# A retention and two-layer feed-forward kernel on one core: the sign of float64 weights found another way, and attention block loads split over two DMA queues

## Chip, core, metric

The kernel runs on one core of one Trainium2 chip. The metric is device microseconds (us) of one execution; the median of three runs is given, and one more execution was profiled. Engines are named as in the profile: PE (matrix multiply), PEld (its weight loads), DVE (vector engine), ACT (scalar engine), POOL (GpSimd), SP (the engine that does nothing here but issue DMAs).

## Reference

The weights are float64, everything else is float32.

```python
def _attn_ref(q, k, v):                       # B=2, H=8, S=768, D=64
    gamma = 1.0 - 2.0 ** (-5.0 - np.arange(H))
    for t in range(S):
        state = gamma * state + k[:, :, t] (outer) v[:, :, t]
        y[:, :, t] = q[:, :, t] @ state / sqrt(D)

def _moe_ref(x, w_in, w_out):                 # x 1536 x 512, w_in 512 x 2048, w_out 2048 x 512
    h = x @ w_in
    return (np.maximum(h, 0.0) + np.log1p(np.exp(-np.abs(h)))) @ w_out

def _moe2_ref(x, w_in, w_out):                # same shapes
    h = x @ w_in
    return (h * np.clip(h + 3.0, 0.0, 6.0) / 6.0) @ w_out

out = _moe2_ref(_moe_ref(attention(q, k, v)))
```

## The kernel before

**Matrix products.** Each layer m (0 or 1) is worked off in steps s = (m, c, f): c is one of 3 chunks of 512 tokens, f one of 16 slices of 128 of the hidden width, 96 steps in all. `gemm1` makes h for a step in one PSUM bank (12 matmuls of 512 columns), ACT and DVE make the activation g from it and split it into a high part `hi` and a low part `lo`, and `gemm2` adds the step's share of the output into four PSUM banks (12 matmuls). A product of two float32 numbers is three products of parts: high by high, high by low, low by high. After the last f of a chunk, ACT and DVE split the four banks into `x_hi` and `x_lo`, the input of the next layer. Below, "a product" is one such group of 12 matmuls.

**Weights.** There are 64 weight tiles (32 a layer), each 128 x 512 float64, 512 KB. `weight(m, o, f, number)` loads one into a `raw` buffer as two 32-bit words for each number and makes the parts in a `cv` buffer: `bits` (ACT) turns the low word into the mantissa's last bits; `sign` (ACT) reads the top 16 bits of the high word and writes a float16 zero with the right sign into the upper half of the same word; the high word, read as a float32, is then scaled by 2^-112 and clamped, either `scale` on ACT and `clamp` on DVE (all of layer 1, and every second tile of layer 0, by `SCALED`) or `scaled` and `capped`, both on DVE (the other 16 tiles of layer 0); `merge` (DVE) shifts it by three bits and ORs it into `cv`. `high` (ACT), and `low` (DVE) or `negative` (ACT) with an accumulating DMA that POOL issues, then write the two parts into a `w` buffer.

**Attention.** The 12 units u of 128 positions come in three kinds. Units 0 to 3 run first. Units 4 to 7 are spread between the first products of layer 0. Units 8 to 11 are spread between later ones, when the 32 weights of layer 0 are done and their `raw` and `cv` buffers serve as attention buffers. For these last four, k and q are loaded as 32 x 32 blocks (`blocks`: 16 DMAs of 16 KB for `kb`, 16 for `qb`), DVE transposes each (`in_blocks`), and q is multiplied by a table. There is one `kb`, one `qb`, one `kT` and one `qT` buffer, so a unit's blocks can be loaded only when DVE has transposed those of the unit before. A unit is three groups of small matmuls on PE: scores S, inner and state products I, and carry C.

**Order.** Nothing is scheduled at run time: each engine works its instructions off in the order written. The class `Plan` writes that order. Every task has an engine, a cost in microseconds, a due time, the tasks that it waits for and the buffers that it takes; the planner takes the task that could start first, or one that could start within `NEAR` of it and is due earlier. A changed cost or dependency so changes the order on all engines, PE's too.

```python
found.append((at, t))
...
first = min(a for a, _ in found)
at, t = min(((a, t) for a, t in found if a <= first + self.NEAR[e]), key=lambda x: (x[1].due, x[1].n))
```

All instructions are recorded under line 44, the helper through which the planner issues them; tiles tell them apart.

Of the kernel before, what the change touches and what calls it, by code (L numbers as in the profile page):

```python
# [10 lines left out]
F32 = mybir.dt.float32  # L11
F32R = mybir.dt.float32r
U32 = mybir.dt.uint32
U16 = mybir.dt.uint16
F16 = mybir.dt.float16
AF = mybir.ActivationFunctionType
ALU = mybir.AluOpType
PSUM = bass.MemoryType.PSUM
P = 128
# [106 lines left out]

PSX, TT, TS, ACP, ACS = 0.61, 0.62, 0.36, 0.49, 0.55
GEMM = 2.73


@with_exitstack
def kernel(ctx, tc, q, k, v, w1_in, w1_out, w2_in, w2_out, table, out):
    nc = Plan(tc)
    B, H, S, D = q.shape
# [4 lines left out]
    NF = DFF // P  # L139
# [12 lines left out]
    HOLD = 8.0  # L152
# [2 lines left out]
    def BY_DVE(n):  # L155
        return n < 6 or n < 2 * NF and n % 4 != 0

    def SCALED(n):
        return n >= 2 * NF or n % 2 == 1

    tc.nc.scalar.preload_act_table_set("softplus")

# [3 lines left out]
    fixed = pool("fixed")  # L166
# [12 lines left out]
    hold = holds.enter_context(tc.tile_pool(name="hold", bufs=1))  # L179
# [42 lines left out]
    half = fixed.tile([P, 1], F32, name="half")  # L222
    three = fixed.tile([P, 1], F32, name="three")
    nc.vector.memset(half, -0.5 + 7.5 * 2.0 ** -12)
    edge = fixed.tile([P, 1], F32, name="edge")
    nc.vector.memset(three, 3.0)
    nc.vector.memset(edge, 32767.5 * 2.0 ** -60)


    G = [(m, c, f) for m in range(2) for c in range(NC) for f in range(NF)]  # L230
    cost = {"Tk": 0.46, "Tq": 0.46, "S": 0.60, "D": 0.60, "C": 0.98, "I": 0.60, "S0": 0.97, "D0": 0.57, "I0": 0.97, "C0": 0.97, "G1": GEMM, "G2": GEMM}
    pe = [("Tk", 0), ("Tq", 0)]
# [12 lines left out]
    n = 0  # L245
# [6 lines left out]
    due, t = {}, 5.0  # L252
# [10 lines left out]
    def w_part(key, i):  # L263
        return at_slot(("w", key))[:, i]

    def weight(m, o, f, number):
        key = m, o, f
        made = conv[0] if m == 0 else []
        use = due[("G2" if o else "G1"), min(m * NC * NF + f, len(G) - LAG)] - 4.0

        def raw():
            return at_slot((f"raw{m}", key))

        def low_word():
            return raw()[:, :, 0]

        def y():
            return raw()[:, :, 1]

        def w():  # L280
            return at_slot((f"cv{m}", key))

        def fetch():
            src = words[m][o]
            if o:
                nc.sync.dma_start(out=raw().rearrange("p n t -> p (n t)"), in_=src[f * P:(f + 1) * P, :])
            else:
                nc.sync.dma_start(out=raw().rearrange("p (k n) t -> p k (n t)", k=KD),
                                  in_=src[:, 2 * f * P:2 * (f + 1) * P].rearrange("(k p) f -> p k f", p=P))

        def bits():
            nc.scalar.activation(w(), low_word(), AF.Relu, scale=2.0 ** -29 * (1 - 2.0 ** -12), bias=half)

        def sign():
            top = raw().bitcast(U16)[:, :, 3]
            to = w().bitcast(F16).rearrange("p (n x) -> p n x", x=2)[:, :, 1]
            nc.scalar.activation(to, top, AF.Identity, scale=-2.0 ** -60, bias=edge)

        def scale():
            nc.scalar.activation(y().bitcast(F32), y().bitcast(F32), AF.Copy, scale=2.0 ** -112)  # L300

        def clamp():
            nc.vector.tensor_scalar(y().bitcast(F32), y().bitcast(F32), -TOP, TOP, ALU.max, ALU.min)

        def scaled():
            nc.vector.tensor_scalar(y().bitcast(F32), y().bitcast(F32), 2.0 ** -112, -TOP, ALU.mult, ALU.max)

        def capped():
            nc.vector.tensor_scalar(y().bitcast(F32), y().bitcast(F32), TOP, None, ALU.min)

        def merge():
            nc.vector.scalar_tensor_tensor(w(), y(), 3, w(), ALU.logical_shift_left, ALU.bitwise_or)

        def high():
            nc.scalar.activation(w_part(key, 0), w().bitcast(F32), AF.Copy)

        def negative():
            nc.scalar.activation(w_part(key, 1), w().bitcast(F32), AF.Copy, scale=-1.0)

        def low():  # L320
            nc.vector.tensor_tensor(w_part(key, 1), w().bitcast(F32), w_part(key, 0).bitcast(F32), ALU.subtract)

        def add():
            nc.gpsimd.dma_start(out=w_part(key, 1).bitcast(F32), in_=w().bitcast(F32), accum_op=ALU.add)

        raw_k, cv_k = (f"raw{m}", key), (f"cv{m}", key)
        cv, part = [(f"cv{m}", cv_k)], [("w", ("w", key))]
        tail = 1.5 if BY_DVE(number) else 7.0
        T["F", key] = t0 = nc.add("SP", 0.45, fetch, due=begin + 15 if number < 1 else use - tail - 8.0, take=[(f"raw{m}", raw_k)], load=1.45 if o else 1.75)
        t1 = nc.add("ACT", 0.65, bits, [t0], use - tail - 3.5, take=cv)  # L330
        t2 = nc.add("ACT", 0.57, sign, [t1], use - tail - 2.9)
        if SCALED(number):
            t3 = nc.add("ACT", 0.57, scale, [t2], use - tail - 2.3)
            t4 = nc.add("DVE", TS, clamp, [t3], use - tail - 1.9)
        else:
            t3 = nc.add("DVE", TS, scaled, [t2], use - tail - 2.3)
            t4 = nc.add("DVE", TS, capped, [t3], use - tail - 1.9)
        t5 = nc.add("DVE", TT, merge, [t4, t2], use - tail - 1.3, give=[raw_k])
        if BY_DVE(number):
            a = nc.add("ACT", ACS, high, [t5], use - 1.5, take=part, give=[cv_k] + made)  # L340
            b = nc.add("DVE", TT, low, [a], use - 0.7, give=[cv_k] + made)
        else:
            n = nc.add("ACT", ACS, negative, [t5], use - tail, take=part)
            b = nc.add("POOL", 0.9, add, [n], use - tail + 1, give=[cv_k] + made, load=1.6)
            a = nc.add("ACT", ACS, high, [n], use - 2.5, give=[cv_k] + made)
        T["W", key] = [a, b]
# [37 lines left out]
    for j in range(2):  # L384
        r = slice(j * HALF, (j + 1) * HALF)
# [3 lines left out]
        nc.tensor.transpose(idle[:, i % NP, :], ident, ident)  # L389

    arena = [("arena", j) for j in range(LATE)]

    part = [slice(j * HALF, (j + 1) * HALF) for j in range(2)]

# [26 lines left out]
    def attend(u):  # L421
        b, i = divmod(u, NCH)
        ph = int(u >= FIRST)
        d = {n: due.get((n, u)) for n in cost}
# [3 lines left out]
        def task(eng, cost, fn, after, when, take=(), give=(), load=0.0, hold=0.0):  # L428
            when -= EDGE * (u < START and eng in ("DVE", "ACT"))
            return nc.add(eng, cost, fn, after, when, [(p, k) for p, k in take], list(give) + mine, load, hold)  # L430

        def tile_of(n):
            return at_slot((n, u))

        def own(n):
            return [(f"{n}{ph}", (n, u))]
# [9 lines left out]
        def blocks(n):  # L446
            def go():
                src = {"qb": q, "kb": k}[n][b, :, i * C:(i + 1) * C, :].rearrange("(p g) (x t) (e d) -> g e t p x d", g=2, x=4, e=2)
                for g in range(2):
                    for e in range(2):  # L450
                        r = slice((2 * g + e) * 32, (2 * g + e + 1) * 32)
                        for p in range(NP):
                            nc.sync.dma_start(out=tile_of(n)[r, p].rearrange("t (x d) -> t x d", x=4), in_=src[g, e, :, p])
            return go

        def load(n, when, parts=1):
# [5 lines left out]
            at = [d["S" if ph else "Tk"] - 9.0 + x / 2 for x in range(3)]  # L462
        ik, iv = load("k", at[0], 2 if u == 0 else 1), load("v", at[2])
        if ph:
            ikb, iqb = (task("SP", 7.2, blocks(n), [], d["S"] - 25.0, take=own(n), load=2.0, hold=HOLD + d["S"] - 30.0) for n in ("kb", "qb"))
        else:
            iq = load("q", at[1])
        if u == START - 1:
# [2 lines left out]
        if u == 0:  # L471
            ready["t"] = nc.add("SP", 0.45, lambda: nc.sync.dma_start(out=tables, in_=table), [], begin - 1, load=0.1)
            t = nc.add("DVE", 0.62, spread_out, [ready["t"]], begin, take=[("e", "wide")])
            t = nc.add("PE", 0.46, wide_turned, [t], 5.2, take=[("bank", ("tqP", 0))], give=["wide"])
# [16 lines left out]
        else:  # L491
            tp = task("PE", cost["Tk"], turned("k"), [ik, ready.get(("o", u - 1)) if u > START else None], d["Tk"], take=[("bank", ("kP", u))])
            kt = task("ACT", ACP, lambda: nc.scalar.activation(tile_of("kT"), bank(("kP", u)), AF.Copy), [tp], d["S"] - 1.0,
                      take=own("kT"), give=[("kP", u)])
# [8 lines left out]
        if whole:  # L503
# [12 lines left out]
            def masked(g):  # L516
                return lambda: nc.vector.tensor_tensor(at_slot(("pw", u))[:, g], bank(sc[g]),
                                                       full.rearrange("p (n t) -> p n t", n=1).to_broadcast([P, NP, C]), ALU.mult)
# [35 lines left out]
            if first:  # L554
                ready["end", u] = task("DVE", 0.42, faded, [dp, ready["t"]], due["C", u + 1] - 2.0, take=[end], give=[end[1], dk])
                n = None
            else:
                c = task("PE", cost["C0"], carry, [qt, ready["end", u - 1]], d["C"], take=[("bank", o[0])], give=[("qT", u), ("end", u - 1)])
                e = task("DVE", 0.42, total, [dp, ready["end", u - 1]], d["C"] + 1.5, take=[end], give=[end[1], dk, ("end", u - 1)])
                ready["end", u] = task("DVE", 0.42, faded, [e], due["C", u + 1] - 2.0, give=[end[1]])  # L560
                n = task("DVE", 0.1, between, [c], d["C"] + 0.5)
            c = task("PE", cost["I0"], inner, pt + [vs, n], d["I"], take=[("bank", o[0])] if first else [],
                     give=[("pw", u), ("vs", u)] + [("ptw", j) for j in range(2)])
        else:
# [46 lines left out]
            def carry():  # L611
                for j in range(int(first), 2):
                    w = at_slot(mid[1] if j else ("end", u - 1))
                    for p in range(NP):
# [4 lines left out]
            n = task("PE", cost["I"], inner, [pt, vs], d["I"], take=[("bank", x) for x in o], give=[("pt", u), ("vs", u)])  # L619
            dp = task("PE", cost["D"], product, [vs, ik, n], d["D"], give=[("k", u)])  # L620
            sm = task("DVE", 0.42, middle, [dp, ready.get(("end", u - 1)) if not first else None], d["C"] - 1.0, take=[mid],
                      give=o + ([] if first else [("end", u - 1)]))
            tot = None
            if not last:
# [4 lines left out]
                     give=[mid[1], ("qT", u)] + ([] if first else [("end", u - 1)]))  # L629
# [15 lines left out]
    for u in range(NU):  # L645
        attend(u)
# [136 lines left out]
```

## Time and profile before

| | |
|---|---|
| median of 3 runs | 594.3 us (594.19 to 595.33) |
| the profiled execution's own time | 594.75 us |
| its span, first to last instruction | 593.0 us |
| mean granted TensorE clock | 0.996 |
| PE busy / PEld busy | 580.7 us (98%) / 474.1 us (80%) |
| ACT busy / DVE busy / POOL busy | 338.9 us (57%) / 302.0 us (51%) / 34.4 us (6%) |
| DMA, mean over the span | 97 GB/s |

Busy time is the time in which an engine had an instruction in work. A matmul's record is longer than its distance to the next one, since matmuls are pipelined, so that PE's busy share hides short waits; the start times of matmuls show them. The share of an engine over the whole span is a mean over stages: the conversion of layer 0's weights fills ACT and DVE in the first fifth of the span, that of layer 1's fills ACT in the second half of it, and the last third has none.

### The profile page before, as it was taken

The page shows a single profiled execution, that of the slowest core. Times are in us where ns is not written, and L with a number is a line of the kernel's source. Part 1 is how long each engine was busy: PE and PEld are TensorE (multiplying, and loading weights), DVE is VectorE, ACT ScalarE, POOL GpSimd, SP SyncE. Part 2 cuts the span into 40 slices and gives each one's busy share as a digit, 9 for nine tenths or more (in the row PEclk, how much of TensorE's full clock was granted, in tenths as well). Part 3 has the DMA queues.
Part 4 walks back from the last instruction along what each step waited for, and adds up shares of the span by engine and source line. Part 5 has one row for each costly group of instructions (what it writes and reads, how often), then busy time and mean ns, then how long its engine had stood idle before and what let it go on. Part 6 is the DMA issues. An engine that isn't in the chain of part 4 may idle for free.

```text
span 593.0 us, 9082 instructions
## 1 busy us (share of the span) xinstructions
PE 580.7 (98%) x3607; PEld 474.1 (80%) x3607; DVE 302.0 (51%) x531; ACT 338.9 (57%) x552; POOL 34.4 (6%) x46
## 2 busy tenths in 40 slices
PE   8999999999999899999999999999999999999997
PEld 7777877788777688888888788878888888888886
DVE  5998998776556333554555654452412222422223
ACT  3599999974323133788999999962212222222220
POOL 0000010000000000011111122210000000000000
PEclk9999999999999899999999999999999999999999
DMA  9998587513323410156567678720100000100001
GB/s 199 247 269 218 168 209 224 142 19 65 65 33 65 114 38 0 31 131 159 148 147 184 161 198 212 180 50 1 72 0 1 0 1 0 72 0 1 1 1 71
DMA packets 80763, 57.76 MB, mean 97 GB/s; under 512 B 53712, under 2 KB 70352, under 8 KB 80720
## 3 DMA queue, kind: packets, MB, share of 16 engines
q1 hardware_dynamic: 75248, 47.21, 29.1%
q0 software_dynamic: 5472, 9.96, 9.9%
q8 instruction: 28, 0.46, 0.3%
q14 instruction: 15, 0.12, 0.1%
HBM read 44.05 MB, written 3.15 MB: 80 GB/s over the span
## 4 chain that ended last, share of the span: by engine, by line
PE 52%; issue 18%; ACT 18%; DVE 4%; POOL 3%; SPq 3%; DMA 2%; POOLq 0%; DVEq 0%; ACTq 0%
PE banks L44 52%; ACT cv L44 8%; ACT w L44 4%; POOL w L44 3%; SPq L44 3%; ACT raw L44 2%; ACT e L44 1%; ACT hi L44 1%; DVE cv L44 1%; ACT g L44 1%; DMA w<-cv 1%; DVE raw L44 1%; DMA raw<-in_v_dram 1%; DVE g L44 0%; DMA out_dram<-e 0%
## 5 line engine op out<-in xcount | busy, mean ns | idle before, releaser
L44 PE MATMUL banks<-x_hi,w 128*128 128x512 f32 x768 | 253.6, 392 | 0.8 <-ACT w L44 0.3
L44 PEld LDWEIGHTS banks<-x_hi,w 128*128 128x128 f32 x768 | 144.0, 188 | 33.0 <-DVE g L44 1.1
L44 PE MATMUL banks<-x_lo,w 128*128 128x512 f32 x384 | 149.1, 389 | 0.0
L44 PE MATMUL banks<-hi,w 128*128 128x512 f32 x384 | 128.7, 397 | 0.0
L44 PE MATMUL banks<-w,hi 128*128 128x512 f32 (+1 forms) x386 | 118.5, 389 | 1.1 <-DVE x_lo L44 1.1
L44 ACT ACTIVATE e<-banks,three 128x512 f32<-128x512 f32 x48 | 32.8, 684 | 114.5 <-PE banks L44 107.1
L44 DVE TENSOR_TENSOR lo<-g,hi 128x512 fp32r<-128x512 f32 x96 | 66.2, 690 | 53.7 <-ACT hi L44 53.7
L44 DVE SCALAR_TENSOR_TENSOR g<-e,banks 128x512 f32<-128x512 f32 x48 | 33.1, 689 | 113.7 <-ACT e L44 113.4
L44 PEld LDWEIGHTS banks<-hi,w 128*128 128x128 f32 x384 | 72.8, 190 | 16.4 <-ACT hi L44 0.8
L44 PEld LDWEIGHTS banks<-w,hi 128*128 128x128 f32 x386 | 72.2, 188 | 16.7 <-DVE x_lo L44 1.9
L44 ACT ACTIVATE hi<-g 128x512 fp32r<-128x512 f32 x96 | 60.1, 626 | 43.9 <-DVE g L44 41.3
L44 PEld LDWEIGHTS banks<-x_lo,w 128*128 128x128 f32 x384 | 72.1, 188 | 14.6
L44 PE MATMUL banks<-lo,w 128*128 128x512 f32 x192 | 75.9, 395 | 0.5 <-DVE lo L44 0.5
L44 PE MATMUL banks<-w,lo 128*128 128x512 f32 (+1 forms) x193 | 74.9, 388 | 0.0
L44 ACT ACTIVATE w<-cv 128x512 fp32r<-128x512 f32 x102 | 61.2, 622 | 3.8 <-DVE cv L44 3.5
L44 ACT ACTIVATE cv<-raw,edge 128x512 f16<-128x512 uint16 x64 | 55.9, 880 | 1.4
L44 ACT ACTIVATE g<-banks 128x512 f32<-128x512 f32 x48 | 28.1, 586 | 45.9 <-PE banks L44 45.8
L44 POOL DMA_DIRECT2D w<-cv x38 | 33.4, 878 | 358.0 <-ACT w L44 346.7
L44 DVE TENSOR_SCALAR raw<-raw 128x512 f32<-128x512 f32 x80 | 33.9, 427 | 37.4 <-ACT raw L44 33.1
L44 ACT ACTIVATE cv<-raw,half 128x512 uint32<-128x512 uint32 x64 | 48.1, 756 | 1.7 <-DMA raw<-in_moe_w_out_dram 1.1
L44 DVE SCALAR_TENSOR_TENSOR cv<-raw,cv 128x512 uint32<-128x512 uint32 x64 | 43.9, 689 | 1.3
L44 PEld LDWEIGHTS banks<-lo,w 128*128 128x128 f32 x192 | 36.4, 189 | 8.7 <-DVE lo L44 1.5
(59 smaller groups left out, 359.7 us busy)
## 6 DMA issues: line engine op xcount, KB each, us to landing
raw<-in_moe_w_in_dram SPq DMA_DIRECT2D x32, 512.0 KB, 4.1
raw<-in_moe_w_out_dram SPq DMA_DIRECT2D x32, 512.0 KB, 3.7
w<-cv POOLq DMA_DIRECT2D x38, 256.0 KB, 4.1
out_dram<-e SPq DMA_DIRECT2D x11, 256.0 KB, 2.0
q<-in_q_dram SPq DMA_DIRECT2D x8, 256.0 KB, 5.4
v<-in_v_dram SPq DMA_DIRECT2D x8, 256.0 KB, 5.9
k<-in_k_dram SPq DMA_DIRECT2D x7, 256.0 KB, 5.6
raw<-in_k_dram SPq DMA_DIRECT2D x64, 16.0 KB, 1.8
```

The lines of the kernel that those rows point to most:

```text
L44: return self.plan.tc.keep_in_program_order(getattr(self.engine, op)(*args, **kwargs))
```

## The change

The high word is read as an integer (`sign`) where its sign is wanted; ACT no longer scales layer 0's words; in layer 1 ACT takes no part in the sign, which DVE ORs in with a mask (`masked`) after the clamp; and a part of each unit's block DMAs is issued by POOL instead of SP. The constant `edge` goes. `late_sign` is not reached, as `DIRECT` is always true.

```diff
+SIGN = 0.75
...
-    def SCALED(n):
-        return n >= 2 * NF or n % 2 == 1
+    def DIRECT(n):
+        return True
...
         def sign():
-            top = raw().bitcast(U16)[:, :, 3]
-            to = w().bitcast(F16).rearrange("p (n x) -> p n x", x=2)[:, :, 1]
-            nc.scalar.activation(to, top, AF.Identity, scale=-2.0 ** -60, bias=edge)
+            nc.scalar.activation(to(), y().bitcast(I32), AF.Copy, scale=2.0 ** -100)
...
+        def masked():
+            nc.vector.scalar_tensor_tensor(w(), y(), 0x80000000, w(), ALU.bitwise_and, ALU.bitwise_or)
...
         t1 = nc.add("ACT", 0.65, bits, [t0], use - tail - 3.5, take=cv)
-        t2 = nc.add("ACT", 0.57, sign, [t1], use - tail - 2.9)
-        if SCALED(number):
-            t3 = nc.add("ACT", 0.57, scale, [t2], use - tail - 2.3)
-            t4 = nc.add("DVE", TS, clamp, [t3], use - tail - 1.9)
+        if m:
+            t2 = nc.add("ACT", 0.57, scale, [t0], use - tail - 3.0)
+            t3 = nc.add("DVE", TS, clamp, [t2], use - tail - 2.5)
+            t4 = nc.add("DVE", TT, masked, [t3, t1], use - tail - 2.0)
         else:
-            t3 = nc.add("DVE", TS, scaled, [t2], use - tail - 2.3)
-            t4 = nc.add("DVE", TS, capped, [t3], use - tail - 1.9)
-        t5 = nc.add("DVE", TT, merge, [t4, t2], use - tail - 1.3, give=[raw_k])
+            t2 = nc.add("ACT", SIGN, sign, [t1], use - tail - 2.9) if DIRECT(number) else None
+            t3 = nc.add("DVE", TS, scaled, [t0, t2], use - tail - 2.7)
+            t3 = nc.add("DVE", TS, capped, [t3], use - tail - 2.3)
+            t4 = t2 or nc.add("ACT", SIGN, late_sign, [t1, t3], use - tail - 1.9)
+        t5 = nc.add("DVE", TT, merge, [t3, t4], use - tail - 1.3, give=[raw_k])
...
+    SHARE = {"kb": 2, "qb": 1}
...
                         for p in range(NP):
-                            nc.sync.dma_start(out=tile_of(n)[r, p].rearrange("t (x d) -> t x d", x=4), in_=src[g, e, :, p])
+                            (nc.gpsimd if p > SHARE[n] else nc.sync).dma_start(out=tile_of(n)[r, p].rearrange("t (x d) -> t x d", x=4), in_=src[g, e, :, p])
...
-            ikb, iqb = (task("SP", 7.2, blocks(n), [], d["S"] - 25.0, take=own(n), load=2.0, hold=HOLD + d["S"] - 30.0) for n in ("kb", "qb"))
+            ikb, iqb = (task("SP", 0.48 * 4 * (SHARE[n] + 1), blocks(n), [], d["S"] - 25.0, take=own(n), load=2.0, hold=HOLD + d["S"] - 30.0) for n in ("kb", "qb"))
```

The planner charges SP for the DMAs that it keeps and POOL for none.

What the change does to the order, first on SP and POOL where units 8 and 9 are loaded (`raw_0` holds `kb` and `qb`; of the other rows, `raw_1` and `raw_2` are the unit's k and v). SP before:

```order
L44 DMA raw_1_70<-in_moe_w_out_dram 128x1024
L44 DMA raw_0_69<-in_k_dram 32x4x32 x16
L44 DMA raw_0_69<-in_q_dram 32x4x32 x16
L44 DMA raw_1_70<-in_k_dram 128x8x64
L44 DMA raw_2_71<-in_v_dram 128x8x64
```

SP now, then POOL now:

```order
L44 DMA raw_1_70<-in_moe_w_out_dram 128x1024
L44 DMA raw_0_69<-in_k_dram 32x4x32 x12
L44 DMA raw_0_69<-in_q_dram 32x4x32 x8
L44 DMA raw_1_70<-in_k_dram 128x8x64
L44 DMA raw_2_71<-in_v_dram 128x8x64
```

```order
L44 DMA w_1303<-cv_3_77 128x512
L44 DMA raw_0_69<-in_k_dram 32x4x32 x4
L44 DMA raw_0_69<-in_q_dram 32x4x32 x8
L44 DMA raw_0_69<-in_k_dram 32x4x32 x4
L44 DMA raw_0_69<-in_q_dram 32x4x32 x8
```

Each unit's 32 block DMAs are now 20 on SP and 12 on POOL, where they stand between the last accumulating DMA of layer 0's weights and the first of layer 1's.

On PE, around the first block unit (`cv,cv` rows are S and I, `st` rows C, each other row the first of the matmuls of one product). Before:

```order
L44 MATMUL banks<-hi_106,w_81 128x512
...
L44 MATMUL banks<-x_hi_618,w_82 128x512
...
L44 MATMUL banks<-hi_108,w_83 128x512
...
L44 MATMUL banks<-cv_1_75,cv_0_74 64x64 x16
L44 MATMUL banks<-x_hi_618,w_84 128x512
```

Now:

```order
L44 MATMUL banks<-hi_106,w_81 128x512
...
L44 MATMUL banks<-cv_1_75,cv_0_74 64x64 x16
L44 MATMUL banks<-x_hi_602,w_82 128x512
...
L44 MATMUL banks<-cv_3_77,cv_2_76 64x64 x16
...
L44 MATMUL banks<-cv_1_75,st_135 64x64 x8
...
L44 MATMUL banks<-cv_1_75,cv_0_74 64x64 x16
```

S of unit 8 stands two products earlier: 36 products stand ahead of it, not 38. S of units 9, 10 and 11 now stand behind 39, 44 and 50 products (before: 42, 47 and 51); the last row here is S of unit 9, three products behind that of unit 8.

On DVE, at the end of layer 0's conversion (`raw_1`, `cv_3` and `w` belong to the last weight; the first STREAM_TRANSPOSE is unit 8's k, the second its q). Before:

```order
L44 TENSOR_SCALAR raw_1_70<-raw_1_70 128x512
L44 SCALAR_TENSOR_TENSOR cv_3_77<-raw_1_70,cv_3_77 128x512
...
L44 TENSOR_TENSOR x_lo_259<-banks,x_hi_249 128x512
L44 STREAM_TRANSPOSE cv_0_74<-raw_0_69 128x512
L44 TENSOR_TENSOR x_lo_259<-banks,x_hi_249 128x512 x2
L44 TENSOR_TENSOR lo_111<-g_105,hi_108 128x512
```

Now:

```order
L44 TENSOR_SCALAR raw_1_70<-raw_1_70 128x512
...
L44 TENSOR_SCALAR raw_1_70<-raw_1_70 128x512
L44 SCALAR_TENSOR_TENSOR cv_3_77<-raw_1_70,cv_3_77 128x512
...
L44 STREAM_TRANSPOSE cv_0_74<-raw_0_69 128x512
L44 TENSOR_TENSOR x_lo_257<-banks,x_hi_247 128x512 x3
L44 SCALAR_TENSOR_TENSOR g_105<-g_105,e_102 128x512
L44 STREAM_TRANSPOSE cv_1_75<-raw_0_69 128x512
L44 TENSOR_TENSOR cv_1_75<-cv_1_75,tq_sb 128x512
L44 TENSOR_TENSOR lo_111<-g_105,hi_108 128x512
```

The last weight has one more DVE instruction; the transpose of q has moved ahead of the `lo` that stood before it.

## Rows read from the trace of the kernel before

**Rows 1.** Busy time by stage; then granted clock, DMA engines' share, GB/s.

```profile
core 0: us, PE busy (x) PEld busy (x) DVE busy (x) ACT busy (x) POOL busy (x), PEclk, DMA share, GB/s
22.00:128.00 106.00, 104.89 (x940) 83.04 (x939) 94.40 (x182) 102.58 (x171) 5.52 (x6) 1.00 0.72 192
128.00:198.00 70.00, 67.48 (x636) 53.99 (x634) 39.10 (x69) 24.48 (x41) 0.00 (x0) 1.00 0.32 58
198.00:205.00 7.00, 6.92 (x95) 5.34 (x96) 3.37 (x7) 1.26 (x2) 0.00 (x0) 0.76 0.36 96
...
240.00:396.00 156.00, 154.64 (x679) 126.77 (x679) 82.62 (x143) 145.05 (x239) 27.84 (x32) 1.00 0.63 152
```

**Rows 2.** PE in order of time, to unit 11's S: start, length, idle before.

```profile
195.09 0.39 PE L44 MATMUL banks<-x_hi,w 128*128 128x512 f32 x1
198.09 0.69 PE L44 MATMUL banks<-cv,cv 64*64 64x64 f32 x32 [2.61 <-DVE cv L44]
```

**Rows 3.** SP's DMA issues in order of time: blocks of units 8, 9 and 11.

```profile
124.59 7.45 SPq L44 DMA_DIRECT2D raw<-in_k_dram  x16
...
140.85 8.84 SPq L44 DMA_DIRECT2D raw<-in_k_dram  x16
...
186.46 8.54 SPq L44 DMA_DIRECT2D raw<-in_q_dram  x16
```

**Rows 4.** DVE in order of time: ahead of unit 8's k; units 8 and 11's q.

```profile
137.43 0.69 DVE L44 TENSOR_TENSOR x_lo<-banks,x_hi 128x512 fp32r<-128x512 f32 x1 [0.19 <-ACT x_hi L44]
...
145.38 0.70 DVE L44 STREAM_TRANSPOSE cv<-raw 128x512 f32<-128x512 f32 x1
146.12 0.69 DVE L44 TENSOR_TENSOR cv<-cv,tq_sb 128x512 f32<-128x512 f32 x1
...
196.59 0.71 DVE L44 STREAM_TRANSPOSE cv<-raw 128x512 f32<-128x512 f32 x1 [3.42 <-DMA raw<-in_q_dram]
```

**Rows 5.** DMA issues of the whole span: count, size, median us to landing.

```profile
w<-cv POOLq DMA_DIRECT2D x38, 256.0 KB, 4.1
...
raw<-in_q_dram SPq DMA_DIRECT2D x64, 16.0 KB, 1.8
```

**Rows 6.** PE in order of time: the 37th product, S of units 8 and 9.

```profile
144.07 0.39 PE L44 MATMUL banks<-x_hi,w 128*128 128x512 f32 x1
...
149.61 0.69 PE L44 MATMUL banks<-cv,cv 64*64 64x64 f32 x32
...
163.97 0.69 PE L44 MATMUL banks<-cv,cv 64*64 64x64 f32 x32
```

**Rows 7.** POOL in order of time, three of its 38 DMA issues.

```profile
47.94 1.03 POOL L44 DMA_DIRECT2D w<-cv  x1 [46.28 <-ACT w L44]
...
362.69 0.86 POOL L44 DMA_DIRECT2D w<-cv  x1 [1.64 <-PE banks L44]
363.78 0.88 POOL L44 DMA_DIRECT2D w<-cv  x1 [0.23 <-issue]
```

**Rows 8.** Groups from 22 to 128 us: count, us busy, mean ns, idle before.

```profile
L44 DVE TENSOR_SCALAR raw<-raw 128x512 f32<-128x512 f32 x46 | 19.3, 426 | 5.4 <-ACT cv L44 3.4 <-ACT raw L44 1.2
...
L44 ACT ACTIVATE cv<-raw,edge 128x512 f16<-128x512 uint16 x31 | 26.9, 882 | 0.6
L44 ACT ACTIVATE cv<-raw,half 128x512 uint32<-128x512 uint32 x31 | 23.2, 758 | 0.0
...
L44 ACT ACTIVATE raw<-raw 128x512 f32<-128x512 f32 x16 | 10.7, 669 | 0.2
```

**Rows 9.** Groups from 240 to 396 us.

```profile
L44 ACT ACTIVATE cv<-raw,edge 128x512 f16<-128x512 uint16 x32 | 28.1, 879 | 0.8
...
L44 DVE SCALAR_TENSOR_TENSOR cv<-raw,cv 128x512 uint32<-128x512 uint32 x32 | 22.1, 690 | 0.7
```

**Rows 10.** The change of layers in order of time, ACT and PE.

```profile
333.45 0.60 ACT L44 ACTIVATE x_hi<-banks 128x512 fp32r<-128x512 f32 x1
...
334.95 0.74 PE L44 MATMUL banks<-w,hi 128*128 128x512 f32 x2 [1.13 <-DVE x_lo L44]
```

More of the change, by code (lines that the diff above doesn't have):

```diff
@@ L13 @@
 U32 = mybir.dt.uint32
-U16 = mybir.dt.uint16
+I32 = mybir.dt.int32
 F16 = mybir.dt.float16
@@ L224 @@
     nc.vector.memset(half, -0.5 + 7.5 * 2.0 ** -12)
-    edge = fixed.tile([P, 1], F32, name="edge")
     nc.vector.memset(three, 3.0)
-    nc.vector.memset(edge, 32767.5 * 2.0 ** -60)
     G = [(m, c, f) for m in range(2) for c in range(NC) for f in range(NF)]
@@ L292, in bits, with to, late_sign @@
             nc.scalar.activation(w(), low_word(), AF.Relu, scale=2.0 ** -29 * (1 - 2.0 ** -12), bias=half)
+        def to():
+            return w().bitcast(F16).rearrange("p (n x) -> p n x", x=2)[:, :, 1]
         def sign():
-            top = raw().bitcast(U16)[:, :, 3]
-            to = w().bitcast(F16).rearrange("p (n x) -> p n x", x=2)[:, :, 1]
-            nc.scalar.activation(to, top, AF.Identity, scale=-2.0 ** -60, bias=edge)
+            nc.scalar.activation(to(), y().bitcast(I32), AF.Copy, scale=2.0 ** -100)
+        def late_sign():
+            nc.scalar.activation(to(), y().bitcast(F32), AF.Copy)
+        def masked():
+            nc.vector.scalar_tensor_tensor(w(), y(), 0x80000000, w(), ALU.bitwise_and, ALU.bitwise_or)
         def scale():
```

## Prediction

> **What bounds the kernel now.** I read the stages first. PE is busy 104.9 of 106 us while layer 0's weights are converted and 154.6 of 156 us while layer 1's are [rows 1], so PE's own work is nearly the whole span: a change to the other engines is worth what PE waits for them, a few microseconds at most. The reader is to see in the same rows that the two conversions load different engines. In the first, ACT works 102.6 us and DVE 94.4 us of 106: both are nearly full. In the second, ACT works 145.1 and DVE 82.6 of 156. So ACT stands nearest to the limit in both, but PE hardly waits in either.
>
> Then I read PE in order of time for its largest wait. It stands ahead of S of unit 11: the product before it should have released PE about 0.23 us after 195.09 (matmuls follow each other at about that distance; a product of 12 takes 2.77 us, since two of them lie between 144.07 and 149.61 [rows 6]), and S starts at 198.09 [rows 2]: 2.77 us lost. The wait's cause is two steps back: DVE's transpose of unit 11's q started at 196.59, after 3.42 us of waiting for the q blocks [rows 4], and SP issued these 16 DMAs from 186.46 to 195.00 [rows 3]. They land 1.8 us after an issue [rows 5]. So issuing is the limit: a DMA takes SP 0.47 us (7.45/16) at unit 8 and 0.55 us (8.84/16) at unit 9 [rows 3]. The DMA engines themselves are busy 32% of the time from 128 to 198 us [rows 1].
>
> Right behind this wait the granted clock is down, a mean of 0.76 from 198 to 205 us [rows 1], that is part of the stretch at the lower of the two levels, 1.2 instead of 2.4 GHz. At full clock the same work would have taken 7 x 0.76 = 5.3 us: 1.7 us more lost. The third loss is at the change of layers: 1.13 us of PE waiting for `x_lo`, behind an `x_hi` that ACT began only at 333.45 [rows 10].
>
> **Block loads on two queues.** Removed from SP are 12 of 32 issues a unit, 12 x 0.47 to 12 x 0.55 = 5.6 to 6.6 us; over units 9 to 11 SP gets some 18 us ahead of the 3 us by which unit 11 was late. Its k and v loads, queued behind the blocks, come earlier too. Added to POOL are 12 issues a unit. POOL has nothing else in that stretch (no busy time from 128 to 198 us [rows 1]; its next task is layer 1's first accumulating DMA).
>
> No POOL issue of a small load from DRAM is in the trace. The nearest are its accumulating DMAs: 0.86 us each, 1.09 us from start to start in the one pair that follows closely [rows 7]. I take 1.09 us, with bounds of 0.86 (no gap) and 1.26 (the longer 1.03 us and the same 0.23 us gap). Landing lies between 1.8 us (SP, 16 KB) and 4.1 us (POOL, 256 KB) [rows 5]; I take 3.0.
>
> The order on PE matters here, because S now comes earlier: S of unit 8 follows 36 products, so at 144.07 instead of 149.61 [rows 6]. S of unit 9 follows three products later; four took 163.97 - 149.61 = 14.36 us with the unit's small matmuls, three take 14.36 - 2.77 = 11.6, so it is at 155.7. Units 10 and 11 then follow after five products (17.1 us) and six (19.9 us). Loading began at 124.59, when the last `raw_0` weight was merged; call that t0, and suppose that it stays.
>
> - Unit 8: POOL's twelfth issue starts at t0 + 11 x 1.09 = 12.0, lands at 15.0, and transpose and multiplication take 146.12 + 0.69 - 145.38 = 1.43 us [rows 4]: ready at t0 + 16.4, wanted at 144.07 = t0 + 19.5. Hidden, 3 us to spare.
> - Unit 9: the `kb` buffer is free when unit 8's k is transposed, behind the first `x_lo`, 137.43 + 0.69 [rows 4] and 0.7 more: t0 + 14.2. Four issues to 18.6; the eighth of q starts at 26.2, lands at 29.2, ready at t0 + 30.7. Wanted at 155.7 = t0 + 31.1. 0.4 us to spare, which is none. SP's part (20 issues at 0.55 from t0 + 14.2, 1.8 to land, 1.43) is ready at 27.9.
> - Unit 10 is wanted at t0 + 48.2 and, with POOL running through, ready by about 44. Unit 11 is wanted at t0 + 68.1, ready by about 64, since `qT` is free only after C of unit 10.
>
> So the wait at unit 11 goes (-2.8) and, as nothing follows a long wait, the clock's loss too (-1.7). What is late next is unit 9. With 0.86 and 1.8 us it has some 4 us to spare; with landing at 4.1 it waits 0.6; with 1.26 (POOL then reaches unit 9 only at t0 + 15.1) it waits 2.3. I charge +0.3.
>
> A rule speaks against this part. The trace shows that POOL's issue at 47.94 took 1.03 us, while DVE was 89% busy, and the close pair 0.86 and 0.88 [rows 1, 7]: 0.17 us more at worst. The Trainium skill, "SBUF — State Buffer", section "SBUF: two separate sides", says that a DMA issued from GpSimd has its descriptors written over a port pair that VectorE locks in its two-port modes, and tells of a 620 ns DMA that took 3100 ns that way. In block loading only one single-source SBUF to SBUF instruction of 0.43 us falls in each two products. By the rows the charge stays +0.3; by the rule in full, with every third POOL issue held for 0.43 us, an issue takes 1.23 us and unit 9 waits some 1.6 us.
>
> **Sign and scale in layer 0.** Sixteen ACT scalings go: 10.7 us [rows 8]. Thirty-two signs read a 32-bit word without the bias tile. No such form is in the trace; the nearest rows are the scaling, 0.669 us (32-bit words at the same step, no bias tile), and the old sign, 0.882 us (same float16 output) [rows 8]. I take the middle, 0.78: 3 us less. DVE gets a second instruction for 16 tiles: 16 x 0.426 = 6.8 us [rows 8], so 101.2 of 106 us; ACT falls to 102.6 - 13.7 = 88.9. The fuller of the two goes from 97% to 95%, so I expect the stage to end at the same time, and PE's 1.1 us of waiting in it [rows 1] to stay: 0. The cover for the 6.8 us is DVE's 11.6 us of idle time; only some 4.6 us of that is idle ahead of these very instructions while ACT is behind [rows 8]. Without cover it would cost up to 6.8 us. A gain is bounded by the 1.1 us.
>
> **Two masks in layer 1.** ACT loses 32 signs, 28.1 us, and is left with 117 of 156; DVE gets 32 masks of the same kind as the merge, 22.1 us, and has 104.7 of 156 [rows 1, 9]. PE had 1.4 us of waits there. The clamp no longer stands behind the sign. Both engines have room, and ACT should come to `x_hi` sooner: of the 1.13 us at the change of layers I take back 0.8 (bounds 0 and 1.3).
>
> **Sum.** -2.8 - 1.7 + 0.3 + 0 - 0.8 = -5.0 us. The profiled execution took 594.75 us (span 593.0, and 1.75 around it, which the change leaves alone), 0.45 above the median of 594.3. It becomes 589.75, the median 589.3.
>
> **Rivals.** (a) *Unit 9 waits for POOL, and only part is gained.* An issue of 1.25 to 1.37 us makes PE wait 2.1 to 4.7 us at unit 9, in place of the 0.3; gain 3.2 to 0.6, time 591.1 to 593.7. For it: the planner charges POOL nothing, so it placed S by SP's part alone. Against: the one close pair of rows.
>
> (b) *POOL issues too slowly: slower than before.* From 1.4 us an issue it decides: unit 8 is then late by 0.3 us, unit 9 by 5.2, together the whole gain. At 1.5 us units 8, 9 and 10 wait 1.4 + 6.4 + 0.9 = 8.7 us: 594.3 - 5.0 - 0.3 + 8.7 = 597.7. For it: the load from DRAM is another form than the accumulation. Against: no issue in the trace is over 1.03 us.
>
> (c) *DVE becomes the limit of layer 0's conversion.* If little of its idle time can be used, weights come up to 6.8 us later, and t0 with them: 594.3 - 5.0 + 6.8 = 596.1; with half covered, 592.7. For it: DVE also makes `lo`, `x_lo` and the transposes, all in one order. Against: 4.8 us would still be free, and ACT, which it waits for, has 13.7 us more.
>
> (d) *The change does not do what it says*: the clock still falls after a shorter wait, or the integer sign is as slow as the old one and other small waits appear with the new order. Little moves: 594.
>
> **Chances.** Forecast 0.52 (587.4 to 591), (a) 0.17, (b) 0.10, (c) 0.13, (d) 0.08. A measurement of this kernel tells about 0.2%, 1.2 us. The forecast, most of (a) and a little of (c) are faster: 0.70. (d) and parts of (a) and (c) are the same: 0.13. (b) and the rest of (c): 0.17. The range begins at 587, where PE also loses neither the 1.1 us in layer 0 nor anything at the change of layers or unit 9 (-6.9), and ends at 595.5, within (c); above are (b) and the worst of (c).
>
> **What would show it.** Right: no wait over 0.5 us ahead of S of unit 11, granted clock 1.00 there; POOL's block issues 1.0 to 1.15 us apart; DVE over 93% and ACT under 87% busy while layer 0 is converted; the new sign under 0.8 us; DVE's waits for `raw` from ACT gone in layer 1. Wrong: a wait ahead of S of unit 9 or 8 after a transpose that waited for a POOL DMA (a, b); PE waits for `w` or `lo` between 22 and 128 us behind a DVE without gaps (c).

## The result and the profile after

The changed kernel takes 587.75 us (median of 4 runs, 587.43 to 588.27), against 594.57 for the kernel before on the same chip (4 runs, 594.19 to 595.33): a ratio of 0.9885, interval 0.9868 to 0.9902. Two later comparisons, of five and six runs of the changed kernel with eight and ten of the one before, gave 0.9908 (0.9893 to 0.9922) and 0.9904 (0.9877 to 0.9932). The forecast was 589.3. The profiled execution of the changed kernel took 587.75 us, its span is 586.0 (7.0 less), its mean granted clock 0.999.

The same stages as in [rows 1], with the same columns:

```profile
22.00:128.00 106.00, 103.94 (x945) 83.53 (x940) 98.75 (x199) 93.21 (x156) 9.24 (x13) 1.00 0.70 192
128.00:198.00 70.00, 70.00 (x677) 56.18 (x676) 40.27 (x71) 24.31 (x41) 23.43 (x42) 1.00 0.33 66
198.00:205.00 7.00, 7.00 (x75) 5.65 (x74) 2.39 (x5) 1.86 (x3) 0.00 (x0) 1.00 0.50 153
...
240.00:396.00 156.00, 156.00 (x690) 129.18 (x689) 101.81 (x174) 118.50 (x205) 27.87 (x32) 1.00 0.63 152
```

PE's records leave no gap while blocks are loaded (70.00 of 70 us, before 67.48), the clock stays at its upper level from 198 to 205 us, and layer 1's conversion has no PE wait at all (156.00 of 156, before 154.64). In layer 0's conversion ACT is down to 93.21 us and DVE up to 98.75: 88% and 93%, where the prediction had under 87% (missed by a point) and over 93% (just met).

PE in order of time where unit 11's S stood behind 2.61 us of waiting [rows 2]. S follows the product without a wait:

```profile
192.05 0.39 PE L44 MATMUL banks<-hi,w 128*128 128x512 f32 x1
192.37 0.69 PE L44 MATMUL banks<-cv,cv 64*64 64x64 f32 x32
```

The DMA issues for units 8 and 9, SP first, then POOL, in order of time (start, length, count):

```profile
123.81 5.56 SPq L44 DMA_DIRECT2D raw<-in_k_dram  x12
129.41 3.75 SPq L44 DMA_DIRECT2D raw<-in_q_dram  x8
...
138.45 6.32 SPq L44 DMA_DIRECT2D raw<-in_k_dram  x12
144.86 3.70 SPq L44 DMA_DIRECT2D raw<-in_q_dram  x8
```

```profile
124.42 2.32 POOL L44 DMA_DIRECT2D raw<-in_k_dram  x4 [10.48 <-DVE raw L44]
126.74 4.46 POOL L44 DMA_DIRECT2D raw<-in_q_dram  x8
138.82 2.28 POOL L44 DMA_DIRECT2D raw<-in_k_dram  x4 [7.63 <-DVE cv L44]
141.81 4.57 POOL L44 DMA_DIRECT2D raw<-in_q_dram  x8 [0.71 <-DVE cv L44]
```

A POOL issue takes 0.56 to 0.58 us here (4.46/8, 2.32/4). For unit 9 it is done with q at 146.38; SP is done at 148.56. The two queues end within about two microseconds of each other, so neither is far behind. The landing (the median, in us, from an issue until its data has arrived), from the view of the DMA issues:

```profile
raw<-in_q_dram POOLq DMA_DIRECT2D x32, 16.0 KB, 2.2
raw<-in_q_dram SPq DMA_DIRECT2D x32, 16.0 KB, 2.0
```

There is one new long wait. PE in order of time, at the eighth product:

```profile
52.19 0.40 PE L44 MATMUL banks<-x_lo,w 128*128 128x512 f32 x1
53.96 0.73 PE L44 MATMUL banks<-x_hi,w 128*128 128x512 f32 x2 [1.38 <-DMA w<-cv]
```

This product's weight (tile 8) gets its low part through ACT and an accumulating DMA of POOL; in the new order the product stands one place earlier, and PE meets the DMA before it has landed. Against that, four waits that the kernel before had at 27, 45, 101 and 113 us (0.4 to 0.6 us each) are gone, and two of 0.7 and 0.3 us at 29 and 34 us have come.

The new sign and its neighbours, groups from 22 to 128 us, against [rows 8]; and the two mask operations and the scaling of layer 1, groups from 240 to 396 us, against [rows 9]:

```profile
L44 DVE TENSOR_SCALAR raw<-raw 128x512 f32<-128x512 f32 x62 | 26.0, 427 | 2.4 <-ACT cv L44 1.8
...
L44 ACT ACTIVATE cv<-raw 128x512 f16<-128x512 int32 x31 | 24.5, 791 | 0.4
```

```profile
L44 DVE SCALAR_TENSOR_TENSOR cv<-raw,cv 128x512 uint32<-128x512 uint32 x64 | 44.0, 689 | 1.3
...
L44 ACT ACTIVATE raw<-raw 128x512 f32<-128x512 f32 x32 | 21.1, 660 | 0.0
```

DVE's clamp waited long for ACT in layer 1, and still waits a little. The same stretch before, then after:

```profile
L44 DVE TENSOR_SCALAR raw<-raw 128x512 f32<-128x512 f32 x32 | 13.7, 428 | 31.9 <-ACT raw L44 31.9
```

```profile
L44 DVE TENSOR_SCALAR raw<-raw 128x512 f32<-128x512 f32 x32 | 13.7, 428 | 8.2 <-ACT raw L44 7.9
```

### The profile page after: what moved, and what is told of

Its sections match the earlier page's. It is cut to its first block, busy times and chain, and to the rows that moved or that the text cites. A ratio compares the mean times of both kernels' runs of the same rounds, so it can differ in the third digit from the quotient of the medians.

```text
span 586.0 us, 9131 instructions
## 1 busy us (share of the span) xinstructions
PE 576.5 (98%) x3607; PEld 473.3 (81%) x3607; DVE 324.8 (55%) x578; ACT 303.2 (52%) x504; POOL 61.6 (11%) x94
## 3 DMA queue, kind: packets, MB, share of 16 engines
HBM read 44.05 MB, written 3.15 MB: 81 GB/s over the span
## 4 chain that ended last, share of the span: by engine, by line
PE 93%; DMA 2%; DVE 2%; ACT 1%; SPq 1%; issue 1%; DVEq 0%; ACTq 0%
PE banks L44 93%; DMA w<-cv 1%; DMA q<-in_q_dram 1%; SPq L44 1%; DVE raw L44 1%; ACT cv L44 0%; DMA out_dram<-e 0%; ACT w L44 0%; DVE cv L44 0%; DVE pw L44 0%; DVE e L44 0%; ACT g L44 0%; DVE w L44 0%; DVE x_lo L44 0%; DVE st L44 0%
## 5 line engine op out<-in xcount | busy, mean ns | idle before, releaser
L44 PE MATMUL banks<-hi,w 128*128 128x512 f32 x384 | 126.8, 392 | 0.0
L44 DVE SCALAR_TENSOR_TENSOR cv<-raw,cv 128x512 uint32<-128x512 uint32 x96 | 65.9, 688 | 1.7
L44 DVE TENSOR_SCALAR raw<-raw 128x512 f32<-128x512 f32 x96 | 40.6, 428 | 10.7 <-ACT raw L44 7.9
L44 PEld LDWEIGHTS banks<-w,lo 128*128 128x128 f32 x193 | 36.3, 188 | 7.4
```

Of the source, the lines that this page charges most:

```text
L44: return self.plan.tc.keep_in_program_order(getattr(self.engine, op)(*args, **kwargs))
```

## The experiments

Eleven kernels ran, in three groups of four, four and three; each group has its own runs of the kernel before (31, 8 and 10). The mean granted clock of each execution splits the kernel before in two. Of its 49 executions 27 had a mean of 0.999 or 1.000 and a median of 593.04 us, and 22 had 0.994 to 0.998 and 594.88 us. The profiled execution [rows 1] is of the second kind: the clock falls behind the wait at unit 11, which is called the dip below. The other executions have no trace; that theirs is the same dip is inferred from their clock. The two kinds lie 1.84 us apart. That need not be the dip alone, since the wait itself may be longer where the clock falls. Where it matters, executions without a dip are compared with executions without one.

**One part alone: layer 0's sign.** The kernel before with this edit:

```diff
-        t2 = nc.add("ACT", 0.57, sign, [t1], use - tail - 2.9)
-        if SCALED(number):
+        if m == 0:
+            t2 = nc.add("ACT", 0.75, new_sign, [t1], use - tail - 2.9)
+            t3 = nc.add("DVE", TS, scaled, [t0, t2], use - tail - 2.7)
+            t3 = nc.add("DVE", TS, capped, [t3], use - tail - 2.3)
+            t5 = nc.add("DVE", TT, merge, [t3, t2], use - tail - 1.3, give=[raw_k])
```

> The kernel before with layer 0's new sign alone (read as an integer, no scaling by ACT); layer 1 and the block loads as before. Theory (the three parts add up, each in its own stage): the time stays, ratio 0.998 to 1.002, 593.3 to 595.7 us; the fuller of ACT and DVE between 22 and 128 us stays near 95%, the wait of 2.6 us ahead of S of unit 11 and the clock's dip behind it stay, PE's waits in layer 0's conversion change place and not sum (within 1.5 us). Rival 1 (ACT's relief in layer 0 is what gained): 589 to 591 us, with t0, the begin of block loading, some microseconds earlier. Rival 2 (DVE's added instructions cost time, and the other parts hide it): 596 us or more.

Measured: 592.53 us, ratio 0.9983 (0.9964 to 1.0002), before 593.88. That alone tells it neither from nothing nor from a small gain. The ratio is in the theory's range, the time is below it (593.3 at least). Without a dip it is 592.07 (8 runs) against 592.88 (16 runs): some 0.8 us less, with ranges that overlap. One pair of traces does not show where that comes from. In it PE reaches S of unit 8, behind the same matmuls, no sooner (149.80 us, before 149.61), but block loading began 25.44 us ahead of that S, before 25.02. SP is that much less late at unit 11, and in the profiled execution the wait there is shorter and the clock stays up, against the theory. The last kernels below put the gain in layer 0 after all. PE in order of time, then the stage:

```profile
195.28 0.39 PE L44 MATMUL banks<-x_hi,w 128*128 128x512 f32 x1
197.51 0.69 PE L44 MATMUL banks<-cv,cv 64*64 64x64 f32 x32 [1.84 <-DVE cv L44]
198.13 0.50 PE L44 MATMUL banks<-hi,w 128*128 128x512 f32 x1
198.47 0.39 PE L44 MATMUL banks<-lo,w 128*128 128x512 f32 x1
```

```profile
198.00:205.00 7.00, 7.00 (x88) 5.62 (x78) 3.10 (x5) 1.09 (x2) 0.00 (x0) 1.00 0.49 133
```

Rival 1 (589 to 591) and rival 2 (596 or more) both fall.

**One part alone: layer 1's two masks.**

```diff
+        if m == 1:
+            t2 = nc.add("ACT", 0.57, scale, [t0], use - tail - 3.0)
+            t3 = nc.add("DVE", TS, clamp, [t2], use - tail - 2.5)
+            t4 = nc.add("DVE", TT, masked, [t3, t1], use - tail - 2.0)
+            t5 = nc.add("DVE", TT, merge, [t3, t4], use - tail - 1.3, give=[raw_k])
```

> The kernel before with layer 1's two masks alone. Theory: all of PE's waits from 220 to 400 us go, 2.2 us of 37 lost before, and nothing ahead of it changes: 592.3 us (591.8 to 592.9), the wait at unit 11 as before. Rival 1 (the prediction's own size of this term): 0.8 us, 593.7. Rival 2 (layer 1's gain in the changed kernel came from the earlier attention units, not from the masks): 594.4, with the wait of about 1.1 us at the change of layers kept.

Measured: 591.77 us, ratio 0.9977 (0.9954 to 1.0000). Part of the 2.1 us between the medians is chance: 4 of its 10 runs and 15 of the 31 of the kernel before had the dip, so that one median lies among runs without it and the other between the two kinds. Without a dip it is 591.63 (6 runs) against 592.88 (16 runs), 1.25 us less; among runs with a dip it is 0.7 us less (4 and 15 runs). The masks do remove every PE wait of the stage, as the theory had it; rival 2 falls. The size without a dip lies between the theory's (2.2) and rival 1's (0.8). The stage (columns as in [rows 1]):

```profile
240.00:396.00 156.00, 156.00 (x690) 129.18 (x689) 103.12 (x177) 120.69 (x209) 27.88 (x32) 1.00 0.63 152
```

**One part alone: the shared block loads.**

```diff
-                            nc.sync.dma_start(out=tile_of(n)[r, p]...
+                            (nc.gpsimd if p > SHARE[n] else nc.sync).dma_start(out=tile_of(n)[r, p]...
...
-            ikb, iqb = (task("SP", 7.2, blocks(n), ...
+            ikb, iqb = (task("SP", 0.48 * 4 * (SHARE[n] + 1), blocks(n), ...
```

> The kernel before with the block loads shared between SP and POOL alone (with the planner's new charge for them). Theory: the wait at unit 11 (2.8 us) and the clock's dip behind it (1.7 us) go, nothing else: 590.0 us (589.4 to 590.7), POOL's block issues about 0.57 us each as in the changed kernel, granted clock 1.00 from 198 to 205 us. Rival 1 (all three parts are needed together): over 592 us. Rival 2 (all of the gain is in the blocks): 587.7.

Measured: 589.79 us (589.30 to 591.21, ten runs, none with a dip), ratio 0.9943 (0.9923 to 0.9962): 4.1 us less. The time is the theory's; both rivals fall. In its trace PE has no gap up to unit 11, and the clock stays up behind it (columns as in [rows 1]):

```profile
128.00:198.00 70.00, 70.00 (x677) 56.17 (x676) 41.13 (x71) 25.07 (x42) 24.47 (x44) 1.00 0.34 67
198.00:205.00 7.00, 7.00 (x75) 5.65 (x74) 2.14 (x4) 2.10 (x4) 0.00 (x0) 1.00 0.41 126
```

Without a dip on either side it is 3.1 us. So the rest of the median's gain goes with the dip, which came in none of these ten runs. (Of the 15 runs of the changed kernel itself one had a mean clock under 0.999: 0.997, at 590.19 us.)

**The changed kernel without shared loads.** All blocks on SP, and the planner's charge of 7.2 us.

> The changed kernel with all block loads on SP and the planner's old charge of 7.2 us for them: both sign changes without the shared loads. Theory (the parts add up): 592.3 us (591.5 to 593.3), wait of 2 to 3 us ahead of S of unit 11 and the dip behind it as before. Rival (the earlier end of layer 0's conversion already lets SP catch up): no wait ahead of S of unit 11, 588 us.

Measured: 591.57 us, ratio 0.9960 (0.9937 to 0.9983). The time is in the theory's range. The profiled execution waits 1.69 us at unit 11 (clock 1.00), less than the 2 to 3 us of the theory; six of the ten runs have the dip. The rival falls: the block loads stay late without the second queue.

**The order without the queue.** The changed kernel, its planner's charges and so its order kept, once repeated as it is and once with all 32 block loads of a unit on SP:

```diff
-                            (nc.gpsimd if p > SHARE[n] else nc.sync).dma_start(...
+                            nc.sync.dma_start(...
```

> The changed kernel once more, beside the next three on one chip. All theories: 587.8 us (587.3 to 588.3).

> The changed kernel's order on PE, DVE and ACT, with all 32 block loads of a unit issued by SP. Theory (SP's issuing is the limit, and the earlier places of S make it worse): SP needs 32 x 0.47 to 0.55 = 15 to 18 us a unit; unit 8 is just in time (ready at t0 + 18.5, wanted at t0 + 19.5), unit 9 waits 3 to 4 us, unit 11 again 1 to 3 us, with dips of the clock behind: 592 to 596 us. Rival (the new order on PE removed the wait, not the second queue): no wait over 0.5 us ahead of any S from unit 8 on, 587.8 us.

Measured: 588.09 us for the changed kernel, 599.88 us with all on SP, ratio to the kernel before 1.0110 (1.0093 to 1.0127). The second queue is worth 11.8 us in this order, and the order with both sign changes, but on one queue, is 6.3 us slower than the kernel before. It is not the earlier places of S that gain; they need the faster loading. The time is above the theory's range. The wait at unit 9 was 5.2 us, not 3 to 4: the transpose of q, which waits for its loads, stands ahead of `x_lo` on DVE, and `x_lo` ended 0.6 us after q was ready (160.61 and 160.01 us). S of unit 11, where the theory had 1 to 3 us more, does not wait; instead PE waits 2.6 us ahead of unit 10's I, for v, which SP issued only at 184.11, behind 17 loads of k. The clock fell behind both waits; the theory had named such dips without a figure. DVE in order of time, PE in order of time, and PE's stretches of 5 us (columns: busy, clock, DMA share, GB/s):

```profile
158.57 0.71 DVE L44 STREAM_TRANSPOSE cv<-raw 128x512 f32<-128x512 f32 x1 [4.89 <-DMA raw<-in_q_dram]
159.32 0.69 DVE L44 TENSOR_TENSOR cv<-cv,tq_sb 128x512 f32<-128x512 f32 x1
159.93 0.68 DVE L44 TENSOR_TENSOR x_lo<-banks,x_hi 128x512 fp32r<-128x512 f32 x1
```

```profile
155.27 0.39 PE L44 MATMUL banks<-x_hi,w 128*128 128x512 f32 x1
160.66 1.13 PE L44 MATMUL banks<-cv,cv 64*64 64x64 f32 x32 [5.00 <-DVE x_lo L44]
161.73 0.79 PE L44 MATMUL banks<-hi,w 128*128 128x512 f32 x1
162.32 0.63 PE L44 MATMUL banks<-lo,w 128*128 128x512 f32 x1
```

```profile
155.00:160.00 5.00, 0.66 (x3) 0.90 0.48 100
160.00:165.00 5.00, 4.34 (x40) 0.50 0.38 61
165.00:170.00 5.00, 5.00 (x80) 0.92 0.21 34
```

At 0.50, the lower of the two levels, the first two matmuls of the product behind S last 0.79 and 0.63 us. At the upper level, in the same place, they lasted 0.50 and 0.39 (198.13 and 198.47, with layer 0's sign alone).

**All on POOL.** The line above with `nc.gpsimd`.

> The changed kernel's order, with all 32 block loads of a unit issued by POOL. Theory (a POOL issue takes 0.57 us whatever the number in a row): 18.2 us a unit, so that S of unit 8 waits 1 to 2 us, unit 9 some 4 to 6 us, unit 11 again: 593 to 598 us. Rival 1 (POOL's issues of four in a row were short because a queue took them without waiting, and longer rows slow to about 1.0 us): 32 us a unit, waits of over 10 us ahead of S of units 8 to 11, over 615 us. Rival 2 (issuing on POOL is cheaper than on SP and not the limit): 588 us.

Measured: 606.36 us, ratio 1.0212 (1.0191 to 1.0233). Rows of sixteen cost 0.57 us an issue, like rows of four, so rival 1's slowing isn't there, and rival 2 falls as well. POOL in order of time:

```profile
134.69 9.16 POOL L44 DMA_DIRECT2D raw<-in_q_dram  x16
...
182.07 9.16 POOL L44 DMA_DIRECT2D raw<-in_k_dram  x16
191.32 9.16 POOL L44 DMA_DIRECT2D raw<-in_q_dram  x16
```

The theory's issue time holds, its time (593 to 598) was too low. It reckoned the waits of S alone; PE also waits 3.4 us ahead of unit 8's C, because the transpose of unit 9's k stands ahead of unit 8's `st` on DVE and waits for POOL, and 3.6 us ahead of unit 10's I, where the transpose of unit 11's k stands in the way. PE's five waits (2.7, 3.4, 4.8, 0.4 and 3.6 us) are 15 us together, of the 16.8 by which this profiled execution (604.78 us) is longer than the changed kernel's (588.01).

**The new wait taken away.** Weight tile 8 gets its low part from DVE:

```diff
-        return n < 6 or n < 2 * NF and n % 4 != 0
+        return n < 9 or n < 2 * NF and n % 4 != 0
```

> The changed kernel, in which weight tile 8 also gets its low part from DVE instead of by POOL's accumulating DMA. Theory: the wait of 1.4 us ahead of the eighth product, for that DMA's landing, goes, and DVE has room for one more instruction of 0.7 us: 586.4 us (586.0 to 587.0), ratio to the changed kernel 0.996 to 0.999. Rival (PE only meets the next weight sooner, behind a DVE that is 93% busy): the wait returns within the next ten products, 587.5 to 588.2 us.

Measured: 586.81 us (586.25 to 587.26), beside 588.09 for the changed kernel: 1.3 us less, the two ranges apart, and in the theory's range. PE in order of time at the same place:

```profile
51.19 0.69 PE L44 MATMUL banks<-qT,kT 64*64 64x64 f32 x32
51.81 0.50 PE L44 MATMUL banks<-hi,w 128*128 128x512 f32 x1
52.15 0.39 PE L44 MATMUL banks<-lo,w 128*128 128x512 f32 x1
```

No wait, and it does not come back later (PE's loss from 60 to 140 us is 5.4 us; 6.2 in the changed kernel). This version is faster than both kernels. The order changed along with the route: a product of `hi` and `lo` stands in this place again, so what the route and what the place did is not told apart.

**One part undone.** The changed kernel again, then with the old sign in layer 1, then with the old sign and scaling in layer 0 (the reverse of the first two diffs):

> The changed kernel once more, beside the next two on one chip. All theories: 588.1 us (587.4 to 588.7).

> The changed kernel with layer 1's sign as before (ACT makes it, no second mask). Theory (layer 1's waits come back, and only these; kernels with the old layer 1 lost 1.3 to 2.2 us there by their traces): 1.3 to 2.2 us over the changed kernel, 589.4 to 590.3 us. Rival 1 (the prediction's own size): 0.8 us over it, 588.9. Rival 2 (the masks save nothing once the attention units come earlier): within 0.3 us of it.

> The changed kernel with layer 0's sign and scaling as before. Theory (the new sign only moves PE's small waits, and the 0.4 us by which it brings the block loading forward is covered once the loads are shared): 587.4 to 588.7 us, within 0.6 us of the changed kernel; the wait of 1.3 to 1.5 us ahead of the eighth product gone and four waits of 0.4 to 0.6 us back. Rival 1 (the 0.8 to 1.4 us that the new sign gave when it was made alone are its worth here too): 588.9 to 589.5. Rival 2 (it costs, by the new wait): under 587.2.

Measured: 588.18 us (587.82 to 590.19), then 589.58 (588.68 to 590.60) and 588.91 (588.36 to 589.10), six runs each. Layer 1's masks are worth 1.4 us, in the theory's range. Layer 0's part is worth 0.7 us, more than the theory allowed (0.6) and just at rival 1's lower end. The waits of 0.58 and 0.48 us at 102 and 113 us are back with the old sign, and the wait at the eighth product is gone.

The start of S of unit 8 shows where the 0.7 us lie, since the same number of matmuls stands ahead of it in all kernels of one order. In the new order it is 144.26 and 144.73 us with the old sign (the shared loads alone, layer 0 undone), and 143.46 to 144.08 with the new one (five traces in which S does not wait: the changed kernel three times, all on SP, layer 1 undone). In the order of the kernel before it is 149.61 and 150.17 with the old sign (before, layer 1's masks alone), and 149.80 and 148.66 with the new one (layer 0's sign alone, both signs). The means are 0.7 us apart in either order. So the gain is made ahead of unit 8, though traces of one kind lie up to 1.1 us apart; which of the small waits makes it is not settled.

## Why the prediction was right

**The bound.** Right. SP's issuing made unit 11 late; twelve issues a unit moved to POOL remove that (4.1 us alone, 11.8 in the new order). The prediction's figure for the block part, -2.8 - 1.7 + 0.3 = -4.2, is what the shared loads gave alone, in part by luck: without a dip they gave 3.1, and the dip, reckoned in full, adds 1.0 to a median over executions of both kinds.

**The wait at unit 11** (-2.8). Right, in the profiled execution. The same wait is 2.0 us (layer 0's part alone), 1.7 us (both signs) and 3.15 us (layer 1's alone) in the executions profiled of other kernels. SP's issue time varies between them (unit 10's 16 issues for its `kb` took 8.1, 8.1 and 9.9 us in these three), and the new sign in the first two lets SP begin 0.4 us sooner.

**The clock's loss** (-1.7). Near in size (the two kinds of executions lie 1.84 us apart, a longer wait perhaps included) for an execution that has it. The prediction took it for a part of every execution. The three that gave it the median of 594.3 lay high (594.19 to 595.33); the 49 later ones went down to 591.58.

**Unit 9** (+0.3). The price was wrong, and the sign "1.0 to 1.15 us apart" did not come. A POOL block issue takes 0.57 us, not 1.09, and lies below the lower bound of 0.86. That the miss was on the cheap side is luck; the one pair of rows did not tell. The bound came from the accumulating DMAs, which are another form; those still take 0.88 us in the changed kernel. Landing is 2.2 us, nearer to the lower bound (1.8) than to 3.0. So unit 9 waits for nothing, and rivals (a) and (b), which needed 1.25 us and more, had no ground. The Trainium skill, "DMA: Bandwidth & Descriptors", section "Anatomy of one DMA — SWDGE (gpsimd) path", gives about 2.0 us plus bytes over 436 GB/s for a DMA issued there, 2.04 us for 16 KB as an estimate; the 2.2 us of the trace agree, and that figure would have been nearer than the 3.0 taken.

**The rule on DVE and POOL's descriptors**, weighed in the prediction. It shows in the rows, at a small price. The first twelve issues, from 124.42 us, took 0.56 and 0.58 us each while DVE was busy 6.63 of 7 us (124 to 131), and those from 138.82 on 0.57 us. But two of the 48 took 0.2 us more than the rest, and each ended 0.12 us after the end of a DVE TENSOR_SCALAR that had begun 0.2 us into the issue. POOL, then DVE:

```profile
156.65 0.75 POOL L44 DMA_DIRECT2D raw<-in_q_dram  x1
170.43 0.76 POOL L44 DMA_DIRECT2D raw<-in_q_dram  x1
```

```profile
156.86 0.42 DVE L44 TENSOR_SCALAR e<-g 128x512 uint32<-128x512 uint32 x1
170.65 0.43 DVE L44 TENSOR_SCALAR e<-g 128x512 uint32<-128x512 uint32 x1 [0.99 <-ACT g L44]
```

Both repeats of the changed kernel have the same two long issues beside the same instruction. No run took that instruction away, so the cause is argued from these times. By the rule in full every third issue would have been held for 0.43 us; in the rows five of 48 were held, for some 0.5 us in all.

**Layer 0** (0, with bounds of -1.1 and +6.8). The mechanism was right: 0.791 us for the new sign (forecast 0.78), DVE took the 16 more scalings (6.7 us) out of idle time, and PE's waits changed place. The size is a little off, -0.7 us where the prediction had nothing; rival (c), DVE as the limit, fell. ACT fell less than reckoned (to 93.2, not 88.9 us), because its records overlap a little: before, its nine groups in the stretch sum to 116.8 us in 102.6 us of busy time, after, its eight to 104.8 in 93.2. Taking 12.0 us of records away took 9.4 us of busy time, and the prediction had subtracted the first from the second.

**Layer 1** (-0.8, bounds 0 and 1.3). Mis-sized. Undone, it is 1.4 us, just above the upper bound; in executions without a dip, alone, 1.25. The prediction took back most of one wait, the 1.13 us at the change of layers. The runs show that all waits of the stage go, the small ones too. One sign did not come in full: DVE's wait for `raw` from ACT fell from 31.9 to 7.9 us and is not gone.

**The sum.** The predicted -5.0 us goes with the profiled execution of before; that pair differs by 7.0 us. Of it 2.8 + 1.7 are unit 11 and the clock, 2.2 are layer 1's waits in that execution. With the terms as measured one by one the sum is -2.8 - 1.7 + 0 - 0.7 - 1.4 = -6.6. Over all runs of the later two comparisons the gain is 5.5 and 6.2 us. So the mechanism held, and three terms were mis-sized, all to the same side: unit 9, layer 0 and layer 1.

## What to carry to other kernels

When a queue's issuing is what is late, count issues, not bytes: the DMA engines were busy a third of the time, and moving 12 of 32 issues to an idle engine removed the wait, while moving all 32 made new ones. A placement table that moves work earlier is worth having only with the resource that can serve it; the same order with one queue was 11.8 us slower. After any change of order, look for the wait that took a new place, and give that one item another route: one more tile on DVE was worth 1.3 us, about as much as layer 1's masks.

## What the hardware showed unexpectedly

A POOL issue of a 16 KB load took 0.56 to 0.59 us in rows of 4, 8 and 16, about what SP takes in the same stretch (0.46 to 0.63 at units 8 to 11), and less than POOL's own accumulating issues of 256 KB (0.88). Whether size, form or the accumulation makes that difference was not tried.

The clock does not fall behind every wait of a given length. It fell behind 2.77 us in the kernel before, 3.15 us in the one with layer 1's masks, and 2.6 us ahead of unit 10's I with all blocks on SP (a mean of 0.69 from 190 to 195 us). With all blocks on POOL it stayed at 1.00 behind waits of 2.74 us (at 144 us), 3.4 us (at 154 us) and 3.64 us (at 192 us), and fell to a mean of 0.67 from 165 to 170 us behind one of 4.80. The kernel before had the dip in 22 of 49 executions. What decides it stays open.
